# Eight maxima out of the lead-in of an attention-and-MLP kernel into steps of five, and a key block's projection in half pieces

## The chip, the cores and the metric

The kernel runs on one core of a Trainium2 chip (trn2). The metric is the device time of one execution in microseconds (us), the median of several runs. TensorE (PE in the profile) multiplies matrices into PSUM banks of 128 rows by 512 numbers, VectorE (DVE) and ScalarE (ACT) read these banks, GpSimd (POOL) works between arrays in SBUF, and SyncE (SP) issues the transfers.

## The reference: what is computed

The result is x + s · g for x of 2048 rows by 512, all in float32. With xn the layer norm of x:

```python
q = (xn @ wq).reshape(B, S, 32, 16).transpose(0, 2, 1, 3)
k = xn @ wk                                   # one key head of 16
v = xn @ wv                                   # one value head of 16
p = softmax(einsum("bhqd,bkd->bhqk", q, k) * 16 ** -0.5)
s = einsum("bhqk,bkd->bhqd", p, v).transpose(0, 2, 1, 3).reshape(B, S, 512) @ wo
h = xn @ w1 + b1                              # 512 -> 1792
g = silu((h * tanh(softplus(h))) @ w2)        # 1792 -> 512
out = x + s * g
```

The 32 query heads share one head of keys and values. The softmax subtracts each row's maximum, so all scores are needed twice: once for the maxima, once for the exponentials.

## The kernel before

**The work.** Queries are cut into 32 groups v, each of 64 maxima tiles (a tile is 128 queries by 512 keys), and into 512 steps, 16 to a group. The 2048 keys lie in four blocks of 512. K and Q are kept in split form in 64 rows (48 for the maxima of later groups), so that a score or a maximum takes half of the array's rows, and two matmuls in different halves run side by side. In a name like m0_1_24 of TensorE's program 0 is the group, 1 the half, 24 the number within the half; m{v}_{a}_{8..15} need the second key block, 16 to 23 the third, and 24 to 31 the fourth.

**A step** (loop at L1556, `em` at L1563, `waves` at L691) issues on TensorE four score tiles e (`e_one`, matmul L1098, exponentials on ScalarE L1100), as a rule four maxima m for a group some steps ahead (`m_one`, matmul L1119, the reduction on VectorE L1123), some half matmuls xps of a projection (L118 to L120: the products of xn with wq or w1, and others), and closes with the four products pv of two steps earlier (L1187, eight records in the trace). Two instructions that lie in different halves of the array share a slot; full-array ones take a slot alone. Seven slots are the usual step. A step with an odd number of half matmuls has three or five maxima; the fifth of five goes into a bank of the score tiles (`m_one` with `other`). There are three banks for scores, three for maxima, one for pv and one for the projection. When a projection group's twelve or more matmuls are complete, ScalarE empties that one bank (hb L830, or qf L770), and the next group's first matmul waits for it.

**The lead-in** ahead of step 0 is not a loop but a planner (L1458 to L1534). It holds a list of tasks for each engine with a duration, dependencies and the earliest start, and a clock for each engine, `T`; at each turn the operation that can start first is issued. Beside tasks TensorE has three kinds of filling: "M", a pair of maxima, one in each half, if `m_ready` (L1436) finds one whose key block is done (`kready`); "X", three matmuls of a projection (`fill(3)`); and a warm matmul without use (`keep_warm`, L1430) where there is nothing else. For each key block c the tasks are: x transposed (L302) and copied (L320), then for the second to fourth block `k_part` (kq, L336, two halves of 256 columns, 16 records), `k_stage` on ScalarE (vt, L341), `k_sum` on TensorE (kp, L345, one matmul of 512 columns), `k_high` on ScalarE (ks, L356), `k_low` on VectorE (ks, L239), which ends the block, and its values' part (`v_copy` L367, `v_transpose` L372, `v_out` L375). When the 64 maxima of group 0 are there, `c_rows(0)` makes four small operations on VectorE (L1154 to L1166) and eight transfers (L1174) that put the maxima beside the queries, and e0_0, the first score, needs the first four of them. The lead-in ends when the maxima are LEAD = 20 steps ahead, 40 in each half, and that transfer is nearly due:

```python
if cdone[0] is not None and s >= cdone[0] - 0.4 and min(m_next) >= 2 * LEAD:
    break
```

After that each step makes four maxima on average, so the distance stays as it is.

Of the kernel before, what the change touches and what calls it, by code (L numbers as in the profile page):

```python
# [20 lines left out]
P = 128  # L21
# [10 lines left out]
NKT = S // P  # L32
NU = 8 * NC
LEAD = 20
NWARM = 24
E0 = 74
X_US = 13.0
# [30 lines left out]
class Task:  # L68


    def __init__(self, eng, us, fn, deps=(), lat=0.1, at=0.0, prio=0):
        self.eng, self.us, self.fn, self.deps, self.lat, self.at, self.prio = eng, us, fn, list(deps), lat, at, prio
        self.end = None

    def start(self, t):
        if any(d.end is None for d in self.deps):
# [50 lines left out]
def block_kernel(ctx: ExitStack, tc: tile.TileContext, x, wq, wk, wv, wo, w1, b1, w2, out):  # L127
# [200 lines left out]
    kq_of = {}  # L328
    vp_of = {}

    def k_part(c):
        kq = ps_v.tile([P, C], F32, tag="v", name=f"kq{c}")
        for h in range(2):
            z = slice(C // 2 * h, C // 2 * (h + 1))
            for dt in range(NDT):
                pe.matmul(kq[32 * dt:32 * dt + 32, z], wkf[:, dt, P - 32:P], xf_of[c][dt // 2][:, dt % 2, z], start=True, stop=True)  # L336
        kq_of[c] = kq

    def k_stage(c):
        vt_of[c] = sb.tile([P, C], F32, tag=f"y{(2, 3, 1, 2)[c]}", name=f"vt{c}", bufs=1)  # L340
        act.activation(vt_of[c], kq_of[c], AF.Copy)  # L341

    def k_sum(c):
        kp_of[c] = ps_v.tile([P, C], F32, tag="v", name=f"kp{c}")
        pe.matmul(kp_of[c], ksum, vt_of[c], start=True, stop=True)  # L345

    def k_proj(c, dts):
        if 0 in dts:
# [9 lines left out]
    def k_low(c):  # L358
        k = ks[KR, C * c:C * (c + 1)]
        stt(k, f(k), ksgn[KR, 0:1], kp_of[c][KR], ALU.mult, ALU.add)  # L360
        kready[c] = now[0] + 0.85

    def v_copy(c):
        if c == 0:
# [326 lines left out]
    def waves(h, em, new):  # L691

        if not cur["chunk"] and (not new or cur["g"] is None and not begin()):
            mms = []
        else:
            g = cur["g"]
            mms = cur["chunk"] or g.mms[cur["n"]:cur["n"] + chunk_size(len(g.mms) - cur["n"], g.most)]  # L700
        second = bool(cur["chunk"])
        k = len(mms)
        ms = em(k, second)
        a = deque(ms[1 - h])
        b = deque(ms[h])
        ps = cur["ps"]
        ends = second and cur["n"] + k == len(cur["g"].mms)
        xs = deque(mms)
        swap = k % 2 and k > 5 and not second
        relay = None  # L710
        first = True
        done = False
        while a or b or xs:
            if xs:
                i = xs.popleft().half(ps, h)
                if first and cur["relay"] is not None:
                    tc.add_manual_dep(i.ins, cur["relay"].ins.name, mybir.DependencyInfo(
                        mybir.DependencyClass.Sync, mybir.DependencyReason.DATA), reason="other half of the bank")
                first = False
                if ends and cur["g"].dve and len(xs) == HOLD + k % 2:  # L720
                    held[0] = []
                if not xs and ends:
                    cur["n"] += k
                    cur["chunk"] = []
                    finish()
                    done = True
                    for top in held[0] or ():
                        top()
                    held[0] = None
            elif b and not swap:  # L730
                b.popleft()()
            if len(a) > 1 or a and not xs:
                r = a.popleft()()
                if k and not xs and relay is None:
                    relay = r
            if b and swap and not xs and not a:
                b.popleft()()
        if k and not done:
            assert relay is not None
            cur["relay"] = relay  # L740
            if second:
                cur["n"] += k
                cur["chunk"] = []
            else:
                cur["chunk"] = mms
# [356 lines left out]
        return r  # L1102

    m_next = [0, 0]
    behind = deque()

    def m_one(a, other=False):
# [22 lines left out]

    def m_sides(h, k, second):

        tot = 4 + (0 if k % 2 == 0 or k == 5 else -1 if second else 1)
        tot = min(tot, 64 * NU - sum(m_next))
        ahead = m_next[h] - m_next[1 - h]
        lo = max((tot - MLAG - ahead + 1) // 2, tot - (32 * NU - m_next[1 - h]), 0)
        hi = min((tot + MLAG - ahead) // 2, 32 * NU - m_next[h], tot)
        n = (k + tot - 4) // 2 if k % 2 else k // 2
        off = ahead + 2 * n - tot - 2 * h
        if k == 6 and abs(off) > 1:  # L1140
            n -= 1 if off > 0 else -1
        if k == 5:
            n = 2
        n = max(min(n, hi), lo)
        return n, tot - n
# [220 lines left out]
    for c0, c1 in ((0, 1), (1, 2), (2, 3), (3, 4)):  # L1366
# [4 lines left out]
        for c in range(c0, c1):  # L1371
            xs, scs = [], []
            for t in range(4 * c, 4 * c + 4):
                sc = task(*(("ACT", 0.72), ("DVE", 0.4))[c == 0 and t % 2], lambda t=t: x_scale(t), [nrm])
                scs.append(sc)
                tr = task("PE", 0.6, lambda t=t: x_transpose(t), [sc])
                if c == 0:
                    hi = task("ACT", 0.55, lambda t=t: x_high(t), [tr])
                    lo = task("DVE", 0.65, lambda t=t: x_low(t), [hi])
                    xf = task("ACT", 0.62, lambda t=t: x_copy(t), [hi], prio=1)  # L1380
                    if t < 3:
                        bank("e", 3, tr, [lo, xf])
                    xs.append(lo)
                    xs.append(xf)
                else:
                    lo = task("ACT", 0.62, lambda t=t: x_copy(t), [tr])
                    bank("e", 3, tr, [lo])
                    xs.append(lo)

            if c == 0:  # L1390
                def wq_low():
                    if not todo["wq"][0]:
                        split("wq")
                    it = items["wq"][0]
                    sub(dve, it.tile[:, 1], it.raw, f(it.tile[:, 0]))
                xs.append(task("DVE", 0.69, wq_low, scs))

                def q_first():
                    xt_done[0] = step[0]
                    lead["late"] = 2.9  # L1400
                    fill(12)
                    del lead["late"]
            else:
                def keep_x(c=c):
                    xt_keep(c)
                    landed(KEEP_US)
                task("SP", 1.0, keep_x, xs)
            if c == 0:
                qp = task("PE", 2.8, q_first, xs[0:8:2] + xs[8:])
                xs += [qp]  # L1410
            if c == 0:
                k0 = kp = task("PE", 0.9, lambda c=c: k_proj(c, (0,)), xs)
                for dt in range(1, 4):
                    kp = task("PE", 0.9, lambda c=c, dt=dt: k_proj(c, (dt,)), [kp], lat=0.0)
            else:
                kq = task("PE", 1.0, lambda c=c: k_part(c), xs)
                kg = task("ACT", 0.6, lambda c=c: k_stage(c), [kq])
                bank("v", 1, kq, [kg])
                k0 = kp = task("PE", 1.0, lambda c=c: k_sum(c), [kg])
            kv_done = kp  # L1420
            kh = task("ACT", 0.59, lambda c=c: k_high(c), [kp])
            kl = task("DVE", 0.68, lambda c=c: k_low(c), [kh])

            vc = task("ACT", 0.59, lambda c=c: v_copy(c), [kp])
            bank("v", 1, k0, [kl, vc])
            vtr = task("PE", 0.5, lambda c=c: (c == 1 and keep_warm(2), v_transpose(c)), [vc])
            vo = task("DVE", 0.22, lambda c=c: v_out(c), [vtr])
            bank("v", 1, vtr, [vo])
# [5 lines left out]
            pe.matmul(w, qts[2][:, 0, 0:P], qts[2][:, 0], start=True, stop=True)  # L1434

    def m_ready(t):  # L1436
        if min(m_next) >= 2 * LEAD or rows and rows[-1].end is None:
            return None
        v, n = MSEQ[m_next[0]]
        if len(qready.get(v) or ()) <= n % 8 // 4 or n // 8 not in kready:  # L1440
# [17 lines left out]
    while True:  # L1458
# [8 lines left out]
        m = m_ready(T["PE"])  # L1467
        if m is not None and b and b[0] < T["PE"] + 0.2 and T["DVE"] > T["PE"] + 1.0:
            m = None
        if m is not None and (b is None or m <= b[0] + 0.05 or T["DVE"] < T["PE"] + 0.3 and m <= T["PE"] + 0.1):  # L1470
            opts.append((m, "PE", "M"))
        elif b:
            opts.append((b[0], "PE", b[1]))
# [4 lines left out]
        if not any(o[1] == "ACT" and o[0] < T["ACT"] + 0.1 for o in opts):  # L1478
            opts.append((T["ACT"], "ACT", "J"))
        s, e, k = min(opts, key=lambda o: o[0])  # L1480
        if cdone[0] is not None and s >= cdone[0] - 0.4 and min(m_next) >= 2 * LEAD:
            break
        when(s)
        for tag in by_use():
# [21 lines left out]
        elif k == "X":  # L1506
# [5 lines left out]
                kind[0] = "X"  # L1512
            else:
                keep_warm()
                T["PE"] = s + 0.25
                kind[0] = "X"
        elif k == "J":
            tag = next((g for g in ("wq", "ws", "wb") if (g == "wq" or s > 19.0) and arrived(g) and busy[0] + E0 < s + 0.5), None)
# [37 lines left out]
    for s in range(NS + 2000):  # L1556
        inm = s < NS - LEAD
        if inm or cur["chunk"]:
# [78 lines left out]
```

## Time and profile before

| | |
|---|---|
| median of 3 runs | 1576.58 us (1576.44 to 1576.74) |
| the profiled execution | 1576.55 us |
| its span in the trace | 1574.4 us, so 2.15 us lie around it |
| TensorE busy | 1562.6 us, 99% |
| VectorE, ScalarE, GpSimd busy | 85%, 83%, 40% |
| first pair on the second, third, fourth key block | needs ks; the fourth starts at 61.95 us |
| e0_0, the first score | 78.16 us |
| first pv (closes step 2) | 86.26 us |

How to read it: "PE xps L116" is a matmul of TensorE that writes a tile xps at line 116 of the program. A line of the timeline is the start in us, the time from the first start to the last end, the engine, line and operation, output and inputs with their sizes, the number of like instructions in a row, and in brackets how long the engine had been idle and what released it. Matmul ends are modelled and overlap the next start, so times of TensorE are best read from start to start.

### The profile page before, as it was taken

How to read it: one execution, taken by the hardware profiler on the slowest of the kernel's cores; microseconds unless marked ns; L12 is line 12 of the kernel's file. 1: busy time of each engine (PE TensorE's matmuls, PEld its weight loads, DVE VectorE, ACT ScalarE, POOL GpSimd, SP SyncE). 2: the span in 40 equal slices, each digit the busy share in tenths (PEclk: the TensorE clock that was granted, in tenths of full speed). 3: DMA queues.
4: the chain of work that ended last, by engine and by line, in shares of the span. 5: the costliest groups of instructions: out<-in, count | busy, mean ns of one | idle time of the engine just before them, and what ended most of it. 6: DMA issues, size and time to landing. Idle time of an engine off the chain costs nothing.

```text
span 1574.4 us, 31742 instructions
## 1 busy us (share of the span) xinstructions
PE 1562.6 (99%) x11738; PEld 842.0 (53%) x11738; DVE 1341.1 (85%) x2329; ACT 1307.8 (83%) x2518; POOL 633.7 (40%) x683
## 2 busy tenths in 40 slices
PE   9999999999999999999999999999999999999998
PEld 5555555555555555555555555555555555555554
DVE  8998888889889888888998988888889998888832
ACT  7588788798998779878989887887898878789886
POOL 4774266284464105503515320471251515126412
PEclk9999999999999999999999999999999999999999
DMA  6243231232331314122032222211332213032020
GB/s 191 93 124 112 65 101 44 60 118 84 125 97 41 103 44 137 45 69 83 24 100 65 64 93 69 85 59 30 112 99 85 74 40 111 19 111 58 15 81 28
DMA packets 74666, 124.31 MB, mean 79 GB/s; under 512 B 21520, under 2 KB 35344, under 8 KB 74512
## 3 DMA queue, kind: packets, MB, share of 16 engines
q1 hardware_dynamic: 74512, 122.29, 25.2%
q8 instruction: 93, 1.52, 0.4%
q14 instruction: 61, 0.50, 0.1%
HBM read 74.78 MB, written 26.21 MB: 64 GB/s over the span
## 4 chain that ended last, share of the span: by engine, by line
PE 95%; DVE 4%; ACT 1%; DMA 0%; issue 0%; SPq 0%; ACTq 0%; DVEq 0%
PE xps L120 44%; PE pv L1187 32%; PE e L1098 9%; PE m L1119 7%; DVE mb L1123 3%; PE late L120 1%; PE xps L116 0%; ACT pt L1100 0%; DMA xin<-in_dram 0%; PE late L1098 0%; PE kp L351 0%; PE wop L120 0%; PE xp L302 0%; PE late L116 0%; PE wop L116 0%
## 5 line engine op out<-in xcount | busy, mean ns | idle before, releaser
L1123 DVE TENSOR_REDUCE mb<-m 128x1 f32<-128x512 f32 x2048 | 1274.2, 683 | 171.3 <-PE m L1119 152.3
L1100 ACT ACTIVATE pt<-e 128x512 f32<-128x512 f32 x2018 | 1061.6, 602 | 220.7 <-PE e L1098 212.3
L1119 PE MATMUL m<-ks,qt 48*128 48x512 f32 (+1 forms) x2048 | 829.9, 421 | 1.6 <-DVE ks L239 0.5
L1098 PE MATMUL e<-qt,ks 64*128 64x512 f32 x2018 | 740.4, 401 | 0.3
L1187 PE MATMUL pv<-pt,vaug 128*32 128x512 f32 x4096 | 543.0, 604 | 0.0
L1119 PEld LDWEIGHTS m<-ks,qt 48*128 48x128 f32 (+1 forms) x2048 | 372.9, 185 | 55.7 <-DVE mb L1123 18.5
L1098 PEld LDWEIGHTS e<-qt,ks 64*128 64x128 f32 x2018 | 373.3, 186 | 17.9 <-ACT pt L1100 7.5
L120 PE MATMUL xps<-wbs,act 64*128 64x512 f32 x1248 | 339.1, 408 | 0.2
L120 PEld LDWEIGHTS xps<-wbs,act 64*128 64x128 f32 x1248 | 217.7, 185 | 177.4 <-ACT pt L1100 105.8
L120 PE MATMUL xps<-xt,ws 64*128 64x512 f32 x1104 | 305.8, 410 | 0.1
L120 PEld LDWEIGHTS xps<-xt,ws 64*128 64x128 f32 x1104 | 190.6, 185 | 182.7 <-ACT pt L1100 116.5
L174 POOL TENSOR_SCALAR t<-t 128x512 f32<-128x512 f32 x56 | 34.4, 615 | 395.1 <-ACT t L838 394.9
L1187 PEld LDWEIGHTS pv<-pt,vaug 128*32 128x32 f32 x4096 | 81.9, 108 | 137.4 <-issue 129.1
L164 POOL TENSOR_TENSOR hb<-hb,t 128x512 f32<-128x512 f32 x56 | 72.1, 1287 | 65.6 <-ACT t L851 52.4
L120 PE MATMUL xps<-xt,wq 64*128 64x512 f32 x336 | 93.2, 410 | 0.0
L120 PEld LDWEIGHTS xps<-xt,wq 64*128 64x128 f32 x336 | 58.0, 185 | 55.2 <-ACT pt L1100 35.2
L120 PE MATMUL xps<-wbs,ot_all 64*128 64x512 f32 x288 | 79.5, 409 | 0.0
L120 PEld LDWEIGHTS xps<-wbs,ot_all 64*128 64x128 f32 x288 | 49.6, 185 | 46.7 <-ACT pt L1100 29.3
L164 POOL TENSOR_TENSOR hb<-hb,u 128x512 f32<-128x512 f32 x56 | 72.3, 1291 | 4.4
L164 POOL TENSOR_TENSOR u<-u,t 128x512 f32<-128x512 f32 x56 | 71.8, 1282 | 4.7
L164 POOL TENSOR_TENSOR act<-hb,act 128x512 fp32r<-128x512 f32 x55 | 70.8, 1288 | 4.6
L159 POOL TENSOR_SCALAR qh<-qf 128x512 fp32r<-128x512 f32 x15 | 9.3, 620 | 111.8 <-ACT qf L770 76.2
(158 smaller groups left out, 954.9 us busy)
## 6 DMA issues: line engine op xcount, KB each, us to landing
wbs<-w SPq DMA_DIRECT2D x36, 512.0 KB
ws<-w SPq DMA_DIRECT2D x35, 512.0 KB
qt<-qh SPq DMA_DIRECT2D x256, 32.0 KB
w<-wbs SPq DMA_DIRECT2D x14, 512.0 KB
wq<-wq SPq DMA_DIRECT2D x14, 512.0 KB
wbs<-wo SPq DMA_DIRECT2D x12, 512.0 KB
rawws<-in_dram SPq DMA_DIRECT2D x21, 256.0 KB
rawwb<-in_dram SPq DMA_DIRECT2D x20, 256.0 KB
```

The lines of the kernel that those rows point to most:

```text
L120: i = self.pe.matmul(ps, self.lhs()[o], self.rhs()[o], start=(self.k == 0 and self.halves == 0), stop=(self.k == self.tot - 1 and self.hal ...
L159: pool.tensor_scalar(o, i, 1.0, 0.0, op0=ALU.mult, op1=ALU.add)
L164: eng.tensor_tensor(out=o, in0=a, in1=b, op=op)
L174: pool.tensor_scalar(o, o, lim, 0.0, op0=ALU.min, op1=ALU.max)
L1098: pe.matmul(e, ks[o:o + 64, P * k:P * (k + 1)], q[o:o + 64, p], start=True, stop=True)
L1100: r = act.activation(pt, e, AF.Exp, scale=0.25)
L1119: pe.matmul(m, q[o, p, P * t:P * (t + 1)], ks[o, C * kb:C * (kb + 1)], start=True, stop=True)
L1123: r = dve.reduce_max(out=mb_of[v][:, kb, z:z + 1], in_=m, axis=AX.X)
L1187: pe.matmul(o[32 * j:32 * j + 32], vaug[:, k], pt, start=(k == 0), stop=(k == 15))
```

## The change

Four things. (1) `LATER = 4`: the lead-in stops after 36 maxima in each half instead of 40. The eight that are left out are made up in steps: as long as the count is behind, a step from 2 on with 0, 4 or 6 half matmuls has five maxima (`five`), with the scores first in a pair of slots and the rest of the maxima last. (2) The third key block's kq and kp are each two tasks of half the size, and a pair of maxima may go ahead of such a task even where the task could start up to 0.35 earlier (`gap`; 0.05 for all others). (3) kp is written as two matmuls of 256 columns, for the third and for the other two blocks. (4) Two times in the planner are other: a key block counts as ready 0.85 after VectorE's clock rather than after now, and a warm matmul takes 0.42 instead of 0.25.

```diff
+LATER = 4
-    def __init__(self, eng, us, fn, deps=(), lat=0.1, at=0.0, prio=0):
+    def __init__(self, eng, us, fn, deps=(), lat=0.1, at=0.0, prio=0, gap=0.05):
...
-    def k_part(c):
-        kq = ps_v.tile([P, C], F32, tag="v", name=f"kq{c}")
-        for h in range(2):
+    def k_part(c, hs):
+        if 0 in hs:
+            kq_of[c] = ps_v.tile([P, C], F32, tag="v", name=f"kq{c}")
+        kq = kq_of[c]
+        for h in hs:
...
-    def k_sum(c):
-        kp_of[c] = ps_v.tile([P, C], F32, tag="v", name=f"kp{c}")
-        pe.matmul(kp_of[c], ksum, vt_of[c], start=True, stop=True)
+    def k_sum(c, hs):
+        if 0 in hs:
+            kp_of[c] = ps_v.tile([P, C], F32, tag="v", name=f"kp{c}")
+        for h in hs:
+            z = slice(C // 2 * h, C // 2 * (h + 1))
+            pe.matmul(kp_of[c][:, z], ksum, vt_of[c][:, z], start=True, stop=True)
...
-        kready[c] = now[0] + 0.85
+        kready[c] = max(now[0], T["DVE"]) + 0.85
...
-        swap = k % 2 and k > 5 and not second
+        swap = five[0] or k % 2 and k > 5 and not second
...
-        tot = 4 + (0 if k % 2 == 0 or k == 5 else -1 if second else 1)
+        tot = 5 if five[0] else 4 + (0 if k % 2 == 0 or k == 5 else -1 if second else 1)
...
-        if k == 6 and abs(off) > 1:
+        if k == 6 and not five[0] and abs(off) > 1:
...
-                kq = task("PE", 1.0, lambda c=c: k_part(c), xs)
-                kg = task("ACT", 0.6, lambda c=c: k_stage(c), [kq])
-                bank("v", 1, kq, [kg])
-                k0 = kp = task("PE", 1.0, lambda c=c: k_sum(c), [kg])
+                parts = ((0,), (1,)) if c == 2 else ((0, 1),)
+                kq = [task("PE", 0.5 * len(h), lambda c=c, h=h: k_part(c, h), xs, gap=0.35 if c == 2 else 0.05) for h in parts]
+                kg = task("ACT", 0.6, lambda c=c: k_stage(c), kq)
+                bank("v", 1, kq[0], [kg])
+                kp = [task("PE", 0.5 * len(h), lambda c=c, h=h: k_sum(c, h), [kg], gap=0.35 if c == 2 else 0.05) for h in parts]
+                k0, kp = kp[0], kp[-1]
...
-        if min(m_next) >= 2 * LEAD or rows and rows[-1].end is None:
+        if min(m_next) >= 2 * LEAD - LATER or rows and rows[-1].end is None:
...
-        if m is not None and (b is None or m <= b[0] + 0.05 or T["DVE"] < T["PE"] + 0.3 and m <= T["PE"] + 0.1):
+        if m is not None and (b is None or m <= b[0] + b[1].gap or T["DVE"] < T["PE"] + 0.3 and m <= T["PE"] + 0.1):
...
-        if cdone[0] is not None and s >= cdone[0] - 0.4 and min(m_next) >= 2 * LEAD:
+        if cdone[0] is not None and s >= cdone[0] - 0.4 and min(m_next) >= 2 * LEAD - LATER:
...
-                T["PE"] = s + 0.25
+                T["PE"] = s + 0.42
...
             def em(k, second):
+                five[0] = k in (0, 4, 6) and s >= 2 and sum(m_next) < 4 * (LEAD + s)
...
-                for op in EM if k % 2 == 0 or k == 5 or second else EM[::-1]:
+                for op in EM if not five[0] and (k % 2 == 0 or k == 5 or second) else EM[::-1]:
```

The rows below are TensorE's program in order: line, operation, output and inputs, size. First the third key block, before the change. Its kq is one piece of sixteen matmuls, and its kp stands between two pairs of maxima:

```order
L1434 MATMUL warm<-qt_79 128x512 x2
L336 MATMUL kq_611<-xf_0_526,wkf 32x256 x2
L336 MATMUL kq_611<-xf_1_527,wkf 32x256 x2
...
L1119 MATMUL m_0_9_620<-ks,qt_77 128x512
L1119 MATMUL m_1_9_623<-ks,qt_77 128x512
L345 MATMUL kp_629<-vt_626,wkv 128x512
L1119 MATMUL m_0_10_631<-ks,qt_77 128x512
L1119 MATMUL m_1_10_634<-ks,qt_77 128x512
```

And of the change:

```order
L1442 MATMUL warm<-qt_79 128x512 x2
L1125 MATMUL m_0_9_606<-ks,qt_77 128x512
L1125 MATMUL m_1_9_609<-ks,qt_77 128x512
L339 MATMUL kq_613<-xf_0_521,wkf 32x256 x2
L339 MATMUL kq_613<-xf_1_522,wkf 32x256 x2
L1125 MATMUL m_0_10_619<-ks,qt_77 128x512
L1125 MATMUL m_1_10_622<-ks,qt_77 128x512
...
L1125 MATMUL m_0_11_631<-ks,qt_77 128x512
L1125 MATMUL m_1_11_634<-ks,qt_77 128x512
L350 MATMUL kp_638<-vt_629,wkv 128x256
```

Pair 9 moved ahead of kq, pair 10 between its two halves (the second half stands where the rows are cut), and pair 11 ahead of the first half of kp; pair 12 stands between the two halves of kp.

In the fourth block TensorE's program before had, between kp and pair 24, six matmuls of the q projection (wq1) and three warm ones. Now there stand the last three of a group of w1 (ws1), two warm ones, three of the q projection, which open a new group, and three warm ones. The end of the lead-in before:

```order
L1119 MATMUL m1_0_5_985<-ks_98,qt1_78 128x512
L1119 MATMUL m1_1_5_988<-ks_98,qt1_78 128x512
L116 MATMUL xps_959<-xt0_216,early_109 128x512 x3
L1119 MATMUL m1_0_6_996<-ks_98,qt1_78 128x512
L1119 MATMUL m1_1_6_999<-ks_98,qt1_78 128x512
L116 MATMUL xps_1005<-xt0_216,early_109 128x512 x3
L1119 MATMUL m1_0_7_1018<-ks_98,qt1_78 128x512
L1119 MATMUL m1_1_7_1021<-ks_98,qt1_78 128x512
L120 MATMUL xps_1005<-xt0_216,early_109 128x512
L1119 MATMUL m1_1_8_1025<-ks_98,qt1_78 128x512
L120 MATMUL xps_1005<-xt0_216,early_109 128x512
L1098 MATMUL e0_0_1029<-qt0_77,ks_98 128x512
```

And of the change:

```order
L1125 MATMUL m1_0_3_937<-ks_98,qt1_78 128x512
L1125 MATMUL m1_1_3_940<-ks_98,qt1_78 128x512
L117 MATMUL xps_908<-xt0_216,early_109 128x512 x6
L1442 MATMUL warm_952<-qt2_79 128x512
L117 MATMUL xps_964<-xt0_216,early_109 128x512 x12
L117 MATMUL xps_990<-xt0_216,early_109 128x512 x3
L121 MATMUL xps_990<-xt0_216,early_109 128x512
L1125 MATMUL m1_1_4_995<-ks_98,qt1_78 128x512
L121 MATMUL xps_990<-xt0_216,early_109 128x512
L1103 MATMUL e0_0_999<-qt0_77,ks_98 128x512
```

The pairs m1_4 to m1_7 are gone from it, and the projection matmuls, as many before e0_0 as there were, stand together; xps_908, xps_964 and xps_990 are three groups in the one bank. Last, the end of step 5 before:

```order
L1098 MATMUL e5_1_1241<-qt0_77,ks_98 128x512
L120 MATMUL xps_1180<-xt0_216,early_109 128x512
L1119 MATMUL m1_0_19_1246<-ks_98,qt1_78 128x512
L120 MATMUL xps_1180<-xt0_216,early_109 128x512
L1098 MATMUL e5_2_1250<-qt0_77,ks_98 128x512
L1119 MATMUL m1_1_19_1254<-ks_98,qt1_78 128x512
L1098 MATMUL e5_3_1257<-qt0_77,ks_98 128x512
L1187 MATMUL pv0_1130<-pt3_2_1165,vaug_100 32x512
```

And of the change, in a step of five:

```order
L1103 MATMUL e5_1_1226<-qt0_77,ks_98 128x512
L121 MATMUL xps_1162<-xt0_216,early_109 128x512
L1125 MATMUL m1_0_16_1231<-ks_98,qt1_78 128x512
L121 MATMUL xps_1162<-xt0_216,early_109 128x512
L1103 MATMUL e5_2_1235<-qt0_77,ks_98 128x512
L121 MATMUL xps_1162<-xt0_216,early_109 128x512
L1125 MATMUL m1_0_17_1240<-ks_98,qt1_78 128x512
L1103 MATMUL e5_3_1243<-qt0_77,ks_98 128x512
L1125 MATMUL m1_1_16_1247<-ks_98,qt1_78 128x512
L1125 MATMUL m1_1_17_1250<-ks_98,qt1_78 128x512
L1193 MATMUL pv0_1107<-pt3_2_1141,vaug_100 32x512
```

The last two maxima follow the last score, m1_1_17 in a bank of the scores, and the step takes eight slots. Steps 2 to 9 are such steps. The shares of the projection shift with it: step 12 has no half matmul of a projection (steps 13 to 18 have five each), step 19 has eight beside four maxima in ten slots, step 55 again none, and steps 56 and 57 take eight slots each. From the scores of step 58 on the two programs of TensorE are the same.

More of the change, by code (lines that the diff above doesn't have):

```diff
@@ L68 @@
 class Task:
-    def __init__(self, eng, us, fn, deps=(), lat=0.1, at=0.0, prio=0):
+    def __init__(self, eng, us, fn, deps=(), lat=0.1, at=0.0, prio=0, gap=0.05):
         self.eng, self.us, self.fn, self.deps, self.lat, self.at, self.prio = eng, us, fn, list(deps), lat, at, prio
-        self.end = None
+        self.end, self.gap = None, gap
     def start(self, t):
@@ L336, in k_part @@
                 pe.matmul(kq[32 * dt:32 * dt + 32, z], wkf[:, dt, P - 32:P], xf_of[c][dt // 2][:, dt % 2, z], start=True, stop=True)
-        kq_of[c] = kq
     def k_stage(c):
@@ L1104, in block_kernel @@
     m_next = [0, 0]
+    five = [False]
     behind = deque()
```

## The prediction

> **What bounds the kernel now.** I read the page's busy times and its chain of waits, then windows over the stages that the change touches.
>
> ```profile
> span 1574.4 us, 31742 instructions
> PE 1562.6 (99%) x11738; PEld 842.0 (53%) x11738; DVE 1341.1 (85%) x2329; ACT 1307.8 (83%) x2518; POOL 633.7 (40%) x683
> PE 95%; DVE 4%; ACT 1%; DMA 0%; issue 0%; SPq 0%; ACTq 0%; DVEq 0%
> ```
>
> TensorE is the bound over the whole: 99% busy, 95% of the chain. The 4% of VectorE are some 60 us, and they lie where this change works, as the chain around the end of the lead-in shows (start, length, engine and tile):
>
> ```profile
> 51.59 9.65 DVE mb L1123 x16
> ...
> 61.95 0.55 PE m L1119
> ...
> 72.31 0.28 DVE mp L1154
> ...
> 73.25 12.54 DVE mb L1123 x21
> ```
>
> Reductions run back to back (12.54 for 21 is 0.60 each). Windows over the third key block and over the first steps (window, its length, then PE, PEld, DVE, ACT and POOL busy, then the granted clock, 1.00):
>
> ```profile
> 41.30:61.90 20.60, 19.61 (x93) 10.87 (x93) 19.83 (x33) 16.43 (x36) 14.45 (x20) 1.00 0.34 105
> 78.00:86.30 8.30, 7.57 (x44) 3.95 (x42) 8.30 (x16) 6.77 (x13) 7.63 (x8) 1.00 0.37 106
> ```
>
> In both VectorE is busier than TensorE: 19.83 of 20.60, then 8.30 of 8.30. So the lead-in and the first two steps belong to VectorE, all later steps to TensorE. The change takes eight reductions out of the first and puts their matmuls into the second. No work goes: what is gained is what VectorE's queue held up, what is paid is TensorE's slots.
>
> I split the program at three points: the first pair of maxima on the fourth key block (pair 24, at 61.95), the first score matmul e0_0, and the first pv. From the 58th step's scores on, the order of TensorE is the same in both kernels.
>
> **A. Start to pair 24.** Two idle times of VectorE in the third block are what the split is aimed at:
>
> ```profile
> 41.33 1.29 DVE L1123 TENSOR_REDUCE mb<-m 128x1 f32<-128x512 f32 x2 [1.24 <-PE m L1119]
> 43.21 1.29 DVE L1123 TENSOR_REDUCE mb<-m 128x1 f32<-128x512 f32 x2 [0.59 <-PE m L1119]
> ```
>
> With a pair between the pieces both go: 1.24 + 0.59 = 1.83. By VectorE alone pair 24 would come 1.8 earlier. But TensorE is late next:
>
> ```profile
> 58.19 1.13 PE L345 MATMUL kp<-vt,wkv 128*128 128x512 f32 x2
> 60.56 0.85 PE L1434 MATMUL warm<-qt 128*128 128x512 f32 x3
> 61.95 0.50 PE L1119 MATMUL m<-ks,qt 64*128 64x512 f32 x2 [0.53 <-DVE ks L239]
> ```
> ```profile
> 59.36 0.69 ACT L356 ACTIVATE ks<-kp,kone 112x512 fp32r<-112x512 f32 x1 [0.70 <-PE kp L345]
> 60.07 0.59 ACT L367 ACTIVATE vt<-kp 32x512 f32<-32x512 f32 x1
> 75.96 0.69 ACT L830 ACTIVATE hb<-xps,b1c 128x512 f32<-128x512 f32 x1 [3.16 <-PE xps L116]
> ```
>
> The kp of block four moves with VectorE's queue, from 58.19 to 56.36. Behind it the new order puts the last three matmuls of a projection group, two warm ones, then three of the next group, which wait until ScalarE has emptied the one projection bank (hb). On ScalarE that emptying stands behind ks and vt: 56.36 + 1.17 (58.19 to 59.36) + 0.71 (59.36 to 60.07) + about 0.55 for vt + 0.74 (hb at 75.96 lets TensorE go on at 76.70, a row of B) = 59.5. Three projection matmuls at 0.24 and three warm ones (0.85) follow, then pair 24: about 61.05. **Term A −0.9**, between −1.8 (VectorE alone) and −0.4 (one more operation of 0.5 ahead on ScalarE, where a weight's conversion moves up too). On SyncE's queue that weight's load moves ahead of the two stores of the fourth block's x, so it lands earlier than before, and nothing on the path reads those stores.
>
> [...]
>
> ```profile
> 43.10 0.96 PE L116 MATMUL xps<-xt,ws 128*128 128x512 f32 x3
> 43.99 0.50 PE L1119 MATMUL m<-ks,qt 64*128 64x512 f32 x2
> ...
> 72.93 1.66 PE L116 MATMUL xps<-xt,early 128*128 128x512 f32 x6
> 74.53 0.50 PE L1119 MATMUL m<-ks,qt 64*128 64x512 f32 x2
> ```
>
> Three projection matmuls between pairs take 0.89, six take 1.60, so one takes 0.24 and going from the 64-row form to the full one and back takes 0.89 − 0.71 = 0.18. Cutting kq and kp of block three into two pieces adds two such excursions, 0.36, beside VectorE's queue, so nothing in A. [...]
>
> **B. Pair 24 to e0_0.** Before: 61.95 to 78.16, 16.2. Four pairs fewer stand there, but the projection matmuls that filled around them now stand together:
>
> ```profile
> 70.76 0.87 PE L1119 MATMUL m<-ks,qt 64*128 64x512 f32 x4
> 71.61 0.97 PE L116 MATMUL xps<-xt,early 128*128 128x512 f32 x3
> 76.70 0.97 PE L116 MATMUL xps<-xt,early 128*128 128x512 f32 x3 [0.35 <-ACT hb L830]
> 77.93 0.39 PE L120 MATMUL xps<-xt,early 64*128 64x512 f32 x1
> 78.16 0.40 PE L1098 MATMUL e<-qt,ks 64*128 64x512 f32 x1
> ```
> ```profile
> 73.35 5.34 SPq L1174 DMA_DIRECT2D qt<-cr  x8
> ```
>
> To the first of the pairs m1_2 and m1_3 it is 8.8 (61.95 to 70.76) in both. Then two pairs 0.85 (70.76 to 71.61), six projection matmuls with the tail of the last 1.66, the bank's turn 0.75 (ScalarE at 75.96, TensorE on at 76.70), the twelve matmuls of a whole group 1.66 + 6 × 0.24 = 3.1, a second turn 0.75, three matmuls 0.89, and 0.23 for each of two slots (77.93 to 78.16), of which the row of the three covers half of one: 8.8 + 0.85 + 1.66 + 0.75 + 3.1 + 0.75 + 0.89 + 0.2 = 17.0. Before, a pair stood beside each turn. The rows of the maxima for the scores leave VectorE as long after pair 24 as before; their DMA goes out 11.4 after it, and e0_0 could follow within the 4.8 of before (73.35 to 78.16), so by 16.2: TensorE decides. **Term B +0.8**, between 0 and +1.2.
>
> **C. e0_0 to the first pv.** Before:
>
> ```profile
> 86.26 1.06 PE L1187 MATMUL pv<-pt,vaug 128*32 128x512 f32 x8
> ```
>
> 8.1, filled by reductions alone (the second window). Eight fewer wait ahead, so VectorE is idle at e0_0. From e0_0 to this pv TensorE issues some 13 maxima, with three banks for twelve of them. The first reduction starts 0.3 after e0_0 (0.55 behind its matmul by the chain, one slot ahead), the ninth at 0.3 + 8 × 0.60 = 5.1; it ends at 5.7 and lets the twelfth matmul go; one slot later stands the thirteenth, in a score bank, then two turns of slots: pv at about 6.4. **Term C −1.7**, between −2.0 and −1.2.
>
> **D. Seven more steps of five.** Steps 3 to 9 put a fifth maximum into the two halves of the array: eight slots instead of seven. Successive pv mark the steps (two of the usual kind, then steps of eight slots, the last with five maxima, which the old kernel has too):
>
> ```profile
> 94.83 1.06 PE L1187 MATMUL pv<-pt,vaug 128*32 128x512 f32 x8
> ...
> 97.67 1.06 PE L1187 MATMUL pv<-pt,vaug 128*32 128x512 f32 x8
> ...
> 160.72 1.07 PE L1187 MATMUL pv<-pt,vaug 128*32 128x512 f32 x8
> 163.81 1.06 PE L1187 MATMUL pv<-pt,vaug 128*32 128x512 f32 x8
> 166.96 1.06 PE L1187 MATMUL pv<-pt,vaug 128*32 128x512 f32 x8
> ```
>
> Seven slots 2.84, eight 3.09 with four maxima, 3.15 with five. 7 × (3.15 − 2.84) = 2.2. Five reductions of 0.60 are 3.0 in 3.15: VectorE just keeps up. **Term D +2.15**, between 7 × 0.25 = 1.75 (the 3.09) and 7 × 0.34 = 2.4 (the 3.18 of the next fence).
>
> **E. Steps 10 to 58.** Fewer projections done ahead by maxima, and groups shifted by half a step's share: one step runs without projections (12), one step carries eight half pieces with four maxima (19, ten slots), one more empty one comes at 55, then two of eight slots. The old kernel has each kind somewhere (steps 136, 333 and 334):
>
> ```profile
> 470.33 1.06 PE L1187 MATMUL pv<-pt,vaug 128*32 128x512 f32 x8
> 473.05 1.06 PE L1187 MATMUL pv<-pt,vaug 128*32 128x512 f32 x8
> ...
> 1043.02 1.07 PE L1187 MATMUL pv<-pt,vaug 128*32 128x512 f32 x8
> 1046.20 1.06 PE L1187 MATMUL pv<-pt,vaug 128*32 128x512 f32 x8
> 1049.72 1.07 PE L1187 MATMUL pv<-pt,vaug 128*32 128x512 f32 x8
> ```
>
> Against 2.84: step 12, 2.72, −0.1; step 19, 3.52, +0.7; step 55, 3.18, +0.3; four further steps of eight slots at 0.25, +1.0; one more step of five maxima, +0.3. Together +2.2, of which I take **+2.1**, three slots of 0.23 either way: 1.4 to 2.8.
>
> **The sum**, against the profiled execution (span 1574.4 and 2.15 around it, 1576.55; the median of the runs is 1576.58): −0.9 + 0.8 − 1.7 + 2.15 + 2.1 = +2.45, so 1579.0. The corrected time of the fourth block's due date and the 0.42 for a warm matmul cost nothing by themselves: they act through the order, counted above; the warm ones are 39 instead of 40.
>
> **Rivals.** (1) *Slower by over 0.2%* (3.15 us, about what a measurement of this kernel can tell from no change): VectorE takes over in the steps of five. For it: 3.0 of 3.15 is used, and the fifth maximum sits in a bank that the third score of the next step needs. Against it: that score comes a pv and five slots, about 2.2, later, when the queue of at most three reductions (1.8) is gone. It decides from the point where the last reduction ends over 1 us into the next step; then a step costs 3.0 and the 0.55 from matmul to reduction (the chain at 61.95), 7 × (3.55 − 2.84) = 5.0 instead of 2.15: 1581.8. (2) *The better ends*: pair 24 waits for VectorE alone (−1.9), the DMA's bound holds B at 0, C −2.0, D 1.75, E 1.4: −0.65, 1575.9. For it speaks that ScalarE's order may empty the projection bank ahead of vt. [...] (4) *The split brings no pair between*: the order shows that it does, so only its gain could fail; A would be 0 and the time 1579.9.
>
> **Chances.** Forecast 0.60, rival 2 0.21, rival 1 0.08, rival 3 0.02, rival 4 0.09. The range goes from 1575.9, all cheap ends, to 1580.9, the forecast with the dear ends of A, B and E (0.5 + 0.4 + 0.7 and D's 0.25); rivals 1 and 3 stay out. Slower by over 0.2%, above 1579.7, are rivals 1, 3, 4 in part and the upper part of the forecast: 0.20; below 1573.4 0.03; between them 0.77.
>
> **What would show it.** Right: VectorE without the 1.24 and 0.59 in the third block; pair 24 near 61.0; two waits for hb between the last pairs and e0_0, that one near 78.0; first pv near 84.4; steps 3 to 9 at 3.15; steps 12, 19 and 55 at 2.7, 3.5 and 3.2. Wrong: VectorE continuous through steps 3 to 9 with these above 3.3, a granted clock below 1.00 ahead of 25, or later steps that differ though their order doesn't.

## The result, and the profile after

The changed kernel takes 1578.94 us (median of 22 runs, 1578.29 to 1579.41) against 1576.54 (22 runs) for the kernel before: ratio 1.0015, 95% interval 1.0009 to 1.0021. It is 2.4 us slower, and the forecast was 1579.0. The shares of the chain in the profiled execution moved as the argument had it: VectorE has all but left it (4% before, 1% now), and TensorE's share rose from 95% to 97%. From the page of the changed kernel:

```profile
span 1577.1 us, 31733 instructions
PE 1563.3 (99%) x11743; PEld 844.1 (54%) x11743; DVE 1341.4 (85%) x2329; ACT 1307.9 (83%) x2518; POOL 634.0 (40%) x683
PE 97%; DVE 1%; ACT 1%; DMA 0%; issue 0%; SPq 0%; ACTq 0%; DVEq 0%
```

TensorE is busy 0.7 us more, in a span 2.7 us longer. The work is the same but for kp in two pieces and one warm matmul less; it was packed worse. The span grew by 2.7 and the time by 2.4, because 1.8 us lie around the span of this kernel where 2.1 lay around that of the kernel before.

**The lead-in.** VectorE's rows in the third and fourth block of the changed kernel (start, length, operation, then the idle time ahead and what ended it):

```profile
40.12 6.18 DVE L1129 TENSOR_REDUCE mb<-m 128x1 f32<-128x512 f32 x10 [0.37 <-PE m L1125]
...
59.03 0.74 DVE L240 SCALAR_TENSOR_TENSOR ks<-ks,ksgn,kp 112x512 fp32r<-112x512 f32 x1
61.45 2.48 DVE L1129 TENSOR_REDUCE mb<-m 128x1 f32<-128x512 f32 x4 [1.68 <-PE m L1125]
```

Of the idle 1.24 and 0.59 one wait of 0.37 is left, ten reductions follow each other, and ks of the fourth block starts at 59.03 where it was 61.16. But then VectorE stands idle for 1.68 us. TensorE and ScalarE show why:

```profile
56.09 1.13 PE L350 MATMUL kp<-vt,wkv 128*128 128x256 f32 x4
56.87 1.04 PE L117 MATMUL xps<-xt,ws 128*128 128x512 f32 x3
57.75 0.63 PE L1442 MATMUL warm<-qt 128*128 128x512 f32 x2
59.33 0.97 PE L117 MATMUL xps<-xt,wq 128*128 128x512 f32 x3 [0.95 <-ACT hb L835]
60.13 0.85 PE L1442 MATMUL warm<-qt 128*128 128x512 f32 x3
60.92 0.50 PE L1125 MATMUL m<-ks,qt 64*128 64x512 f32 x2
```
```profile
57.25 0.69 ACT L361 ACTIVATE ks<-kp,kone 112x512 fp32r<-112x512 f32 x1 [0.70 <-PE kp L350]
57.97 0.59 ACT L372 ACTIVATE vt<-kp 32x512 f32<-32x512 f32 x1
58.59 0.69 ACT L835 ACTIVATE hb<-xps,b1c 128x512 f32<-128x512 f32 x1
```

Three projection matmuls wait 0.95 for the one projection bank, which ScalarE empties behind ks and vt, and pair 24 stands behind them: 60.92, 1.03 earlier and not 2.1. Then, up to e0_0, the two turns of the bank:

```profile
72.97 3.01 PE L117 MATMUL xps<-xt,early 128*128 128x512 f32 x12 [0.54 <-ACT hb L835]
76.76 0.96 PE L117 MATMUL xps<-xt,early 128*128 128x512 f32 x3 [0.78 <-ACT hb L835]
...
77.99 0.39 PE L1103 MATMUL e<-qt,ks 64*128 64x512 f32 x1
```

e0_0 is 17.07 after pair 24; it was 16.21. The first turn has one warm matmul beside it and the second nothing: with no maxima there, TensorE stands still for 0.54 and 0.78.

**The first steps.** From e0_0 to the first pv it is 6.93 instead of 8.10. TensorE's waits on the way and ScalarE's exponentials:

```profile
80.09 0.50 PE L121 MATMUL xps<-xt,early 64*128 64x512 f32 x1 [0.47 <-ACT pt L1105]
...
82.52 0.50 PE L121 MATMUL xps<-xt,early 64*128 64x512 f32 x1 [0.48 <-ACT pt L1105]
...
84.92 1.07 PE L1193 MATMUL pv<-pt,vaug 128*32 128x512 f32 x8
```
```profile
78.46 2.06 ACT L1105 ACTIVATE pt<-e 128x512 f32<-128x512 f32 x4 [1.76 <-PE xps L121]
80.89 2.06 ACT L1105 ACTIVATE pt<-e 128x512 f32<-128x512 f32 x4 [0.36 <-PE e L1103]
82.81 0.65 ACT L843 ACTIVATE t<-hb 128x512 f32<-128x512 f32 x1
```

VectorE is not what TensorE waits for here any more: both waits end with an exponential (pt), that is, with a free score bank. After the second wait the chain goes through ScalarE once more, by the operation t that stands between two exponentials (start, length, engine and tile):

```profile
82.95 0.51 ACT t L843
83.46 0.50 ACT pt L1105
...
84.00 0.49 PE e L1103
```

**The steps behind.** Rows of pv, one a step: the end of step 4 and of step 5 (a step of five), then step 12 without projections, step 19 with ten slots, step 55 without projections:

```profile
91.30 1.07 PE L1193 MATMUL pv<-pt,vaug 128*32 128x512 f32 x8
94.48 1.07 PE L1193 MATMUL pv<-pt,vaug 128*32 128x512 f32 x8
...
112.94 1.06 PE L1193 MATMUL pv<-pt,vaug 128*32 128x512 f32 x8
115.65 1.06 PE L1193 MATMUL pv<-pt,vaug 128*32 128x512 f32 x8
...
132.85 1.07 PE L1193 MATMUL pv<-pt,vaug 128*32 128x512 f32 x8
136.38 1.07 PE L1193 MATMUL pv<-pt,vaug 128*32 128x512 f32 x8
...
238.60 1.06 PE L1193 MATMUL pv<-pt,vaug 128*32 128x512 f32 x8
241.77 1.07 PE L1193 MATMUL pv<-pt,vaug 128*32 128x512 f32 x8
```

3.18 for a step of five, then 2.71, 3.53 and 3.17.

**All runs by the prediction's terms.** Each number is the difference to the kernel before in one profiled execution. A is counted from the first transpose of x, which begins between 10.10 and 10.69 us after the span's start in these fourteen executions; that is a spread of 0.6 in A if it is left in. "rest" is all behind step 58, where TensorE's order is nearly always the old one. The last columns are the medians of that kernel and of the kernel before in the same set of runs (act_late is a single run). The terms leave out the time around the span: 2.1 us in the kernel before and in warmonly, 1.8 in all others; no run shows why. Against the kernel before, the 95% intervals of later0, nosplit, timesonly, lateronly and warmonly take in no change.

| kernel | A | B | C | D | E | rest | us | before |
|---|---|---|---|---|---|---|---|---|
| the change | −0.93 | +0.86 | −1.17 | +2.35 | +2.04 | −0.35 | 1578.94 | 1576.54 |
| later0 | −0.82 | +0.32 | −0.20 | −0.05 | +0.61 | −0.43 | 1576.18 | 1576.75 |
| later2 | −0.80 | −0.61 | −0.75 | +0.93 | +0.64 | −0.51 | 1575.63 | 1576.75 |
| later6 | −0.81 | +0.88 | −0.72 | +2.48 | +5.74 | +0.10 | 1583.98 | 1576.75 |
| nosplit | −0.62 | −0.42 | −1.28 | +2.30 | +1.42 | −0.16 | 1577.94 | 1576.75 |
| timesonly | −0.57 | −0.07 | +0.07 | −0.04 | +1.28 | +0.09 | 1576.45 | 1576.51 |
| lateronly | +0.02 | −0.43 | −0.70 | +2.31 | −0.28 | −0.20 | 1576.95 | 1576.51 |
| splitonly | −1.68 | −0.09 | +0.05 | −0.04 | +0.69 | +0.15 | 1574.89 | 1576.51 |
| nosplit2 | −0.60 | −0.91 | −0.91 | +0.97 | −0.19 | +0.03 | 1574.22 | 1576.51 |
| warmonly | −0.89 | 0.00 | −0.01 | +0.01 | +0.14 | −0.11 | 1575.56 | 1576.42 |
| splitlater2 | −1.69 | −0.93 | −0.91 | +0.97 | +0.61 | −0.27 | 1574.04 | 1576.42 |
| oldtimes | −1.67 | +0.79 | −1.20 | +2.34 | +1.99 | +0.01 | 1578.16 | 1576.26 |
| act_late | −0.82 | +0.85 | −1.36 | +2.52 | +3.07 | −0.26 | 1580.06 | 1576.42 |

### The profile page after: what moved, and what is told of

It reads as the page before. It is cut to its first block, busy times and chain, and to the rows that moved or that the text cites. A ratio compares the mean times of both kernels' runs of the same rounds, so it can differ in the third digit from the quotient of the medians.

```text
span 1577.1 us, 31733 instructions
## 1 busy us (share of the span) xinstructions
PE 1563.3 (99%) x11743; PEld 844.1 (54%) x11743; DVE 1341.4 (85%) x2329; ACT 1307.9 (83%) x2518; POOL 634.0 (40%) x683
## 4 chain that ended last, share of the span: by engine, by line
PE 97%; DVE 1%; ACT 1%; DMA 0%; issue 0%; SPq 0%; ACTq 0%; DVEq 0%
PE xps L121 44%; PE pv L1193 32%; PE e L1103 9%; PE m L1125 7%; PE xps L117 1%; DVE mb L1129 1%; ACT pt L1105 1%; PE late L121 1%; PE xp L303 0%; PE late L1103 0%; DMA xin<-in_dram 0%; PE kp L350 0%; PE kp L356 0%; PE wop L121 0%; PE kq L339 0%
## 5 line engine op out<-in xcount | busy, mean ns | idle before, releaser
L160 POOL TENSOR_SCALAR qh<-qf 128x512 fp32r<-128x512 f32 x15 | 9.3, 619 | 120.3 <-ACT qf L775 84.9
```

Source lines behind the costliest of these rows:

```text
L160: pool.tensor_scalar(o, i, 1.0, 0.0, op0=ALU.mult, op1=ALU.add)
```

## The experiments

All edits are to the changed kernel; kp stays as two matmuls of 256 columns in all of them.

**later0**: no deferral.

```diff
-LATER = 4
+LATER = 0
```

> The change with LATER = 0: the split of the third block and the two corrected times stay, all 40 maxima of each half are made in the lead-in, no step of five. Theory 1 (the eight deferred maxima cost more slots of TensorE in steps 3 to 58 than VectorE's queue gives back; the split is a gain of its own): pair 24 stays at 60.9, 1.0 earlier than before; the first pv is bound by VectorE again and comes about 1.0 earlier than the 86.26 of before, near 85.2; the steps up to the 58th cost only +0.8 by their slots; in all 0.2 to 0.3 faster than before, about 1576.3 us. Theory 2 (the split and the bank's two turns in the lead-in are what costs, the deferral is harmless): the time stays near the 1578.9 of the change.

Measured: 1576.18, ratio 0.9994 (0.9985 to 1.0002), pair 24 at 61.03, first pv at 85.47. As theory 1 had it: without the eight deferred maxima the loss is gone, and the split doesn't cost.

**nosplit**: no split.

```diff
-                parts = ((0,), (1,)) if c == 2 else ((0, 1),)
+                parts = ((0, 1),)
```

with the two `gap=0.35 if c == 2 else 0.05` as `gap=0.05`.

> The change without the split: kq and kp of the third block are one task each with gap 0.05; LATER = 4 and the corrected times stay. Theory 1: VectorE's idle times of 1.2 and 0.6 in the third block are back and pair 24 is at 61.9 to 62.0 again, 1.0 later than with the change; but the projection groups fall otherwise (one turn of the bank ahead of e0_0 instead of two, and by the slots of steps 3 to 58 +3.6 against before instead of +4.4), so e0_0 comes about 16.0 after pair 24 and the whole is within 0.5 us of the change, about 1578.9. Rival (the 1.0 won at pair 24 is won in the whole time, and the groups' shift is of no weight): 1579.9 to 1580.

Measured: 1577.94, ratio 1.0006 (0.9997 to 1.0015), 1.0 below the change, and pair 24 at 61.16. The expectation missed twice. Pair 24 comes 0.8 earlier than before without any split (0.62 from the first transpose), and taking the split out of the change makes it faster, since B falls from +0.86 to −0.42 and E from +2.04 to +1.42. Something else moves pair 24; the candidates are the two corrected times.

**later2** and **later6**: `LATER = 2`, `LATER = 6`.

> The change with LATER = 2: four maxima deferred instead of eight, three or four steps of five. Theory 1: pair 24 at 60.9; steps 3 to 58 cost +1.8 by their slots (three further steps of five at 0.33, the rest from the shift of the groups); up to the first pv the gain is between that of LATER = 0 and of LATER = 4, about -1.3 to -1.6; in all +0.2 to +0.5, about 1576.9 us. Theory 2 (deferral harmless): near 1578.9, as with LATER = 4.

Measured: 1575.63, ratio 0.9991 (0.9982 to 1.0000): 1.3 lower than expected, about half of it because B is −0.61 and not about 0; −0.51 lies behind step 58. Maxima stand beside some of the projection groups again:

```profile
71.37 0.51 PE L1125 MATMUL m<-ks,qt 64*128 64x512 f32 x2
71.81 0.96 PE L117 MATMUL xps<-xt,early 128*128 128x512 f32 x3
73.55 0.98 PE L117 MATMUL xps<-xt,early 128*128 128x512 f32 x3 [0.78 <-ACT hb L835]
74.46 0.50 PE L1125 MATMUL m<-ks,qt 64*128 64x512 f32 x2
...
76.47 0.49 PE L1103 MATMUL e<-qt,ks 64*128 64x512 f32 x1
```

One turn is paid where the change pays two, e0_0 is at 76.47, and C still brings −0.75. It also shows that e0_0 can come 15.61 after pair 24: the transfer of the maxima is not a bound at 16.2.

> The change with LATER = 6: twelve maxima deferred, steps of five to step 12. Theory 1: nothing more is won up to e0_0, since TensorE and the transfer of the maxima set it; first pv within 0.3 us of that of the change; steps 3 to 58 cost +5.5 instead of +4.4 by their slots; in all about 1.1 above the change, about 1580.0 us. Rival (a longer deferral takes more off VectorE's queue and pays): below 1578.9.

Measured: 1583.98, ratio 1.0048 (1.0035 to 1.0062), 4 more than expected. E is +5.74, of which 3.2 lie in steps 10 to 15. Their pv and VectorE's rows:

```profile
111.30 1.06 PE L1193 MATMUL pv<-pt,vaug 128*32 128x512 f32 x8
115.45 1.06 PE L1193 MATMUL pv<-pt,vaug 128*32 128x512 f32 x8
119.83 1.06 PE L1193 MATMUL pv<-pt,vaug 128*32 128x512 f32 x8
```
```profile
114.04 3.08 DVE L1129 TENSOR_REDUCE mb<-m 128x1 f32<-128x512 f32 x5 [1.07 <-PE m L1125]
118.42 3.08 DVE L1129 TENSOR_REDUCE mb<-m 128x1 f32<-128x512 f32 x5 [1.30 <-PE m L1125]
```

Steps 11 and 12 have five maxima and no projection matmul, and take 4.15 and 4.38. With no projections to fill the slots, the five maxima come behind the scores, VectorE idles over 1 us for the first of them, and its 3.08 for five then cannot be hidden. Price by slots fails for this kind of step, which the kernel before doesn't have.

**timesonly** (the nosplit edit and `LATER = 0`) and **lateronly** (the nosplit edit and the two old times):

```diff
-        kready[c] = max(now[0], T["DVE"]) + 0.85
+        kready[c] = now[0] + 0.85
...
-                T["PE"] = s + 0.42
+                T["PE"] = s + 0.25
```

> Only the two corrected times (and kp as two matmuls of half the columns): no split of the third block, LATER = 0. Theory 1b (what moves pair 24 without the split is the 0.42 for a warm matmul, which puts one warm matmul fewer ahead of the third block's kq): pair 24 near 61.2, as without the split; steps 3 to 58 cost +1.3 by their slots, since the projection groups fall as there; in all +0.4, about 1577.0 us. Rival (the corrected times cost nothing and win nothing, as I first predicted): pair 24 at 61.95, and only the +1.3 remains, 1577.9.

Measured: 1576.45, ratio 0.9999 (0.9990 to 1.0009), pair 24 at 61.01, 0.57 earlier from the first transpose: the corrected times do move it. E gives it back, +1.28 as the slots had it.

> Only LATER = 4 with its steps of five (and kp in two matmuls): no split, old times. Pair 24 at 61.95. Theory 1b (a step of five costs its slot, but the +2 of steps 10 to 58 and the two turns of the bank are the placing of the projection groups, not the deferral): D +2.3, steps 10 to 58 -0.4 by their slots, e0_0 about 15.8 after pair 24, first pv 1.2 closer to e0_0; in all +0.3, about 1576.9 us. Rival, as my prediction had it (the deferral brings D and E together, +4.25, against -0.9 in B and C): 1579 to 1580.

Measured: 1576.95, ratio 1.0003 (0.9994 to 1.0011). D is +2.31, E is −0.28: the deferral by itself brings D, not E. A turn of the bank stands in B here too, with twelve matmuls ahead of it and nine behind, yet B is −0.43:

```profile
71.67 3.02 PE L117 MATMUL xps<-xt,early 128*128 128x512 f32 x12
75.47 2.33 PE L117 MATMUL xps<-xt,early 128*128 128x512 f32 x9 [0.78 <-ACT hb L835]
```

**splitonly** (the two old times, `LATER = 0`).

> Only the split of the third block: old times, LATER = 0. Theory 1b: the idle 1.8 of VectorE goes and pair 24 is limited by TensorE and ScalarE, near 61.0; between kp and pair 24 stand only warm matmuls and no wait for the projection bank; steps 3 to 58 +0.8 by their slots; first pv about 0.8 earlier than before; in all 0.0, about 1576.6 us. Rival (VectorE alone sets pair 24, since no wait for the bank is left): pair 24 at 60.1 and 0.9 less, 1575.7.

Measured: 1574.89, ratio 0.9990 (0.9981 to 0.9998). The rival was right in the cause: pair 24 comes at 59.84, and VectorE sets it; the time is 0.8 below the rival's too.

```profile
57.66 1.65 PE L1442 MATMUL warm<-qt 128*128 128x512 f32 x6
59.84 0.49 PE L1125 MATMUL m<-ks,qt 64*128 64x512 f32 x2 [0.53 <-DVE ks L240]
```

With the old times there stand six warm matmuls where the change has warm ones and three of a new group. No wait for the bank stands ahead of pair 24, and A is −1.68: the split's whole worth.

**nosplit2** (the nosplit edit, `LATER = 2`).

> No split, the corrected times, LATER = 2. Theory 1b: pair 24 near 61.2; no group of projections has to turn the bank without maxima beside it, e0_0 about 15.7 after pair 24; first pv 0.7 closer to e0_0 than before; three steps of five +0.95, two steps without projections -0.3: in all about -1.3, 1575.3 us, the fastest of the set together with LATER = 2 with the split. Rival (the gain of LATER = 2 came from the split): 1576.5 or more.

Measured: 1574.22, ratio 0.9986 (0.9977 to 0.9995); lower than forecast by 1.1. Its two bank turns in B each have a pair of maxima beside them and cost 0.35 each; the second is

```profile
73.59 0.50 PE L1125 MATMUL m<-ks,qt 64*128 64x512 f32 x2
74.44 1.63 PE L117 MATMUL xps<-xt,early 128*128 128x512 f32 x6 [0.35 <-ACT hb L835]
```

**warmonly** (the nosplit edit, `LATER = 0`, and of the times above only `kready` put back).

> Of the two corrected times only the warm matmul's 0.42 (and kp as two matmuls of half the columns); no split, LATER = 0, a key block ready 0.85 after now as before. TensorE's order is that of the kernel before but for a few warm matmuls at the start. Theory 1c (the 0.93 that both times together brought at pair 24 comes from the key block's time, which takes three projection matmuls and a warm one from ahead of the third block): pair 24 at 61.6 to 62.0, first pv at 86.0 to 86.3, the whole within 0.3 of before, 1576.5 us. Theory 1b (it comes from the 0.42): pair 24 at 61.0 and 1575.6 us.

Measured: 1575.56, ratio 0.9993 (0.9985 to 1.0002), pair 24 at 60.85, A −0.89, B to E nearly as before. Theory 1c falls and 1b stands: the 0.42 alone moves pair 24 (kp in two pieces does not, for lateronly has it too, with A +0.02). It does so by issuing fewer warm matmuls in TensorE's queue, one of them in front of the third block's kq. The kernel before, then warmonly:

```profile
38.82 1.05 PE L1434 MATMUL warm<-qt 128*128 128x512 f32 x2
39.80 1.07 PE L336 MATMUL kq<-xf,wkf 128*32 128x256 f32 x16
```
```profile
38.28 0.51 PE L1442 MATMUL warm<-qt 128*128 128x512 f32 x1
38.72 1.07 PE L339 MATMUL kq<-xf,wkf 128*32 128x256 f32 x16
```

Counted from the first transpose, kq starts 0.87 earlier, of which 0.33 was won ahead of this place. Without the split the key block's time brings most of the E of +1.28 (timesonly has it, warmonly has +0.14).

**splitlater2** (the two old times, `LATER = 2`).

> The split, the old times, LATER = 2: the two parts that paid, put together. Theory 1c (the terms add up): pair 24 at 59.85, 2.1 earlier, as with the split alone, since only warm matmuls and no turn of the bank stand ahead of it; e0_0 15.4 to 15.7 after it; first pv 0.8 closer to e0_0 than before; steps 3 to 58 +1.8 by their slots; in all -1.7 to -2.1, about 1574.7 us, level with the best so far. Rival (what the split wins at pair 24 is lost again to the transfer of the maxima ahead of e0_0): e0_0 at 76.4, and 1575.3 or more.

Measured: 1574.04, ratio 0.9984 (0.9975 to 0.9992). The terms add up: A as in splitonly, B and C as in nosplit2, D as in later2. The expected pair 24 of 59.85 came at 60.43 since x began 0.6 later; from the first transpose it is −1.69 against −1.68. Together with nosplit2 it is the fastest of all, 2.4 below the kernel before and 4.9 below the change.

**act_late**: ScalarE's other work out of the first three steps (one execution).

```diff
-            act_jobs(1 + (len(jobs) > 3))
+            if s > 2:
+                act_jobs(1 + (len(jobs) > 3))
```

> The change, but ScalarE takes no operation of the projection's activations beside the exponentials in steps 0 to 2. One look at the stretch from e0_0 to the first pv, 6.93 in the change. If ScalarE's queue sets it there (twelve exponentials at 0.52 and one operation of 0.5, with three score banks), it shrinks to 6.4 to 6.5. If VectorE's queue of maxima sets it, as I predicted, it stays at 6.9. The groups of projections fall otherwise from step 8 on (by slots +5.3 instead of +4.3), so the whole would be near 1579.5 us, which says nothing on this.

Measured: 6.73, between the two. The operation that left is worth 0.2 at most; the second wait is as long without it:

```profile
82.54 0.50 PE L121 MATMUL xps<-xt,early 64*128 64x512 f32 x1 [0.48 <-ACT pt L1105]
```

So, by the chain, what sets this stretch is the exponentials themselves, four of about 0.52 a step over three score banks, and after them TensorE's slots, which here take the place of t on the chain. VectorE's queue is not named in any wait.

**oldtimes** (the two old times, all else as in the change).

> The change with the two old times: split and LATER = 4 stay. Theory (with the corrected times the change puts three projection matmuls of a new group ahead of pair 24, and these wait for the one projection bank; the old times leave only warm ones there): counted from the first transpose of x, pair 24 comes 1.7 earlier than before, as with the split alone, instead of 0.9; e0_0 16.0 to 16.2 after it instead of 17.07, since one group less is turned; first pv as in the change, steps 3 to 58 +4.4 as in the change; in all 1.0 to 1.7 below the change, 1577.2 to 1577.9 us. Rival (the corrected times are a gain here too, as they are without the split): 1579 or more.

Measured: 1578.16, ratio 1.0011 (1.0002 to 1.0020), 0.3 above the range. A is −1.67, as expected, 0.74 better than the change. B is not: +0.79, because a second turn of 0.78 still stands right ahead of e0_0 (at 77.05):

```profile
76.53 0.50 PE L121 MATMUL xps<-xt,early 64*128 64x512 f32 x1 [0.78 <-ACT hb L835]
```

## Why the prediction was right, point by point

**The sum** was right: +2.4 measured between the medians, +2.45 forecast. Four of the five terms were near: A −0.93 (forecast −0.9), B +0.86 (+0.8), D +2.35 (+2.15), E +2.04 (+2.1). C was −1.17 where −1.7 was forecast. The five measured terms come to +3.15, 0.7 above the forecast, and three pieces that the sum put at nothing brought the time back: −0.35 behind step 58, −0.3 around the span (the sum kept the 2.15 of before) and −0.1 in the start of x. The piece behind step 58 ranges from −0.51 to +0.15 in the kernels with nearly the same order there. No run shows what the first two come from, so that the time came out within 0.1 us is luck; with the terms alone it would have been 0.7 off and still inside the range.

**Rival 2's sum** does not add up: with its −1.9 for A the terms give −0.75, not −0.65; the −0.65 belongs to the −1.8 that bounds A.

**A, the wait for the bank**: the mechanism was right, shown by its row (0.95 <-ACT hb) and by oldtimes, where the three matmuls are gone and pair 24 comes 0.74 earlier. Wrong is the step that "the corrected time of the fourth block's due date and the 0.42 for a warm matmul cost nothing by themselves". They act through the order, and A counted only one half of that. In the kernel without a split they bring pair 24 forward by 0.57 (timesonly), and the 0.42 is what does it (−0.89 in warmonly); A had nothing for this. With the split they are what put the three matmuls ahead of pair 24, and these A did count, since it was read from the new order. Little of the missing half is left in the change: kp of the fourth block starts at 56.09 where A had 56.36, and from there to pair 24 each step of the forecast chain holds within 0.1.

**The change of form on TensorE**: a piece of kq took 0.57 (40.01 to 40.58 in the change), two take 1.14, against 1.00 for the whole (39.80 to 40.80 before). So, as an estimate from these starts, it is about 0.14 for the excursion, near the 0.18 worked out. It lay beside VectorE's queue: the split's A of −1.68 (splitonly) against the 1.83 of idle time leaves at most 0.15 for it.

**B**: right in both turns. The bound from the transfer was too high, as later2 shows.

**C**: the step in which the ninth reduction "ends at 5.7 and lets the twelfth matmul go" failed. With eight reductions fewer it is no longer the banks of the maxima that decide in the change but the three score banks: its two waits end with pt, act_late leaves them in place, and VectorE itself waits 0.17 for the ninth maximum behind e0_0, until 83.31. The miss is 0.5, of which at most 0.2 is ScalarE's operation t (act_late, one execution).

**D**: the step of five is 3.18 where I took 3.15 from a step of the old kernel with an odd number of projection matmuls; seven times 0.03 is the miss. VectorE kept up (busy 21.44 of the 22.30 us from 84.9 to 107.2), so rival 1 did not come.

**E**: the steps 12, 19 and 55 took 2.71, 3.53 and 3.17 where 2.72, 3.52 and 3.18 were read from the old kernel. What I did not see is whose cost this is. No single edit owns it; it comes with the places that the projection groups take in the whole order. The deferral of eight alone has −0.28 (lateronly) and the split alone +0.69 (splitonly), but both together have +1.99 (oldtimes). The key block's time adds about 1.1 without the split (timesonly against warmonly) and nothing with it (later0, +0.61).

**Rival 3, the clock** (0.02), a granted clock below 1.00 ahead of 25 us, did not come: from 14.5 to 25 us the granted clock is 1.00 before and 1.00 in the change. The idle time ahead of the first eleven projection matmuls is 0.55 where it was 0.56. The kernel before, then the change:

```profile
14.81 2.83 PE L116 MATMUL xps<-xt,wq 128*128 128x512 f32 x11 [0.56 <-DVE xt L164]
17.47 3.59 PE L351 MATMUL kp<-xf,wkf 128*128 128x512 f32 x8
```
```profile
14.54 2.83 PE L117 MATMUL xps<-xt,wq 128*128 128x512 f32 x11 [0.55 <-DVE xt L165]
17.21 3.60 PE L356 MATMUL kp<-xf,wkf 128*128 128x512 f32 x8
```

The eight matmuls of kp take what they took, 3.6. The longest wait of TensorE quoted here, 0.95, was followed by three matmuls in 0.97, like the 0.96 of others. That a wait lowers the clock was not shown.

## What to carry to other kernels

Deferring work from a stretch that one engine bounds to a stretch that another bounds paid here only up to the point where the first engine falls idle: by the medians, four maxima were a gain (1575.63 in later2, 1574.22 in nosplit2) and eight a loss (1578.94). Around e0_0 VectorE idles for at most 0.33 us at a stretch when four are deferred (later2, nosplit2, splitlater2), for 2.7 to 3.7 when eight are, and for 6.6 with twelve (later6). When an order is made by a planner, compare the whole order after each single edit, since a part of an edit's gain (0.74 of the split's 1.7) can be given back by what another one (the corrected times) puts into the gap. A step's price could be read here from a like step of the old kernel to 0.03 us (3.18 for 3.15); that of a kind that the old kernel lacks could not (4.15 and 4.38 in later6).

## What the runs showed that was not expected

A matmul without use, put in only to keep TensorE busy, was not free here even where TensorE seems to wait: one of them ahead of the third key block and three before that were worth 0.89 at pair 24, and about 0.9 in the whole (warmonly, 1575.56 against 1576.42, whose interval just takes in no change). The turn of the projection bank cost 0.78 where nothing stood beside it (the change, lateronly, oldtimes) and 0.35 beside a pair of maxima (nosplit2). The start of the x transposes differs by up to 0.6 us between the executions shown here, so points of two profiles should be compared from a common event.
